# Gated linear attention with a channel mix on one Trainium2 core: five transfers of SyncE under way in place of eight, for the first 80

## The chip, the cores and the metric

One core of one Trainium2 chip runs the whole kernel. The metric is device time in microseconds (us) of one execution. TensorE is called PE here (PEld for its weight loads), VectorE DVE, ScalarE ACT, GpSimd POOL and SyncE SP. SP computes nothing: it begins DMA transfers, one after the other, in the order of its instructions.

## The reference, cut to what matters

```python
def _attn_ref(q, k, v, f_logit):                 # (4, 8, 768, 48) each
    f = 1.0 / (1.0 + np.exp(-f_logit))
    for t in range(S):
        state = f[:, :, t, :, None] * state + np.einsum('bhd,bhe->bhde', k[:, :, t], v[:, :, t])
        y[:, :, t] = np.einsum('bhd,bhde->bhe', q[:, :, t], state)
    return y

def _moe_ref(x, mu_k, mu_r, w_k, w_v, w_r):      # x: y as (4, 768, 384)
    xk = mu_k * x + (1.0 - mu_k) * x_prev        # x_prev: x one step earlier in time
    xr = mu_r * x + (1.0 - mu_r) * x_prev
    k = np.maximum(xk @ w_k, 0.0)                # 384 x 1024
    v = k * k @ w_v                              # 1024 x 384
    r = 1.0 / (1.0 + np.exp(-(xr @ w_r)))        # 384 x 384
    return r * v
```

The three weight matrices arrive as float64.

## The kernel before

The 4 x 768 time steps are cut into 24 chunks of 128 steps. A chunk is six jobs or more on each engine: its gates are turned into running sums of logarithms, its queries and keys are scaled by them, PE makes the scores and the products with the state, and ACT or DVE brings the result out of PSUM. Three chunks make a unit (eight units, u0 to u7), which then goes through the channel mix: the mix of neighbouring steps (`d`, `xm`), the products with w_k (`F0.0` to `F0.7` for unit 0), the squares, the products with w_r (`R`) and with w_v (`W`), the sigmoid, and the output. Every number that the channel mix multiplies is split into a high and a low part (`xh`, `xl`; `h`, `l`), so each product is three matmuls.

The float64 weights are loaded as pairs of 32-bit words, piece by piece (`wk0` to `wk7`, `wr0` to `wr3`, `wv0` to `wv5`). DVE turns a piece into float32 with three instructions (lines L678, L687 and L690), ACT rounds the high part (L693) and POOL subtracts for the low part (L697). Unit 0 can't start its products before the first pieces of w_k are there.

All of this is one list of tasks in a fixed order: the string `ORDER` names them one by one, `f0.0 sf0.0 cst zT0 ...`, and `emit` (L810) walks through it. Each task's instructions go to one engine, and `emit` ties each instruction to the one before it on its engine, so that no engine's order can change. Waits between engines follow from the tiles that the tasks write and read and are put in by the Tile framework. Transfers are tasks too: `f` (gates, L460), `qk` (a chunk's queries and keys, L234), `v` (values, L236), the weight pieces (L684), `mu` (L773), `sp` (SBUF to SBUF, `x<-stage`, L505), `out` (L652) and `c` (weight words read once more for a check, L745). All but the last output are begun by SP.

The first 30 transfers of SP, in order, are: f0.0, wr2, wk2, wr0, f0.1, f0.2, qk0, f1, wv1, v0, qk1, wk3, v2, wk0, wk4, mu, v1, qk2, wr3, wk6, qk3, wv2, v3, wk1, f2, qk4, wv0, wr1, v4, qk5. The text counts them so: the 8th transfer is f1, the 18th qk2. The 31st is the first `x<-stage`, for unit 0.

The framework gives the transfers of SP eight semaphores in turn, and a transfer that takes a semaphore waits until the one that had it before has landed. So the k-th transfer is begun no earlier than the landing of the (k-8)-th.

A second way of computing (`general`) is in the program for inputs with very strong gates. It doesn't run on these inputs, and its lists are emitted with `pinned=False`.

Of the kernel before, what the change touches and what calls it, by code (L numbers as in the profile page):

```python
# [45 lines left out]
WORDS = {"wk": (-0.282, 0.023), "wr": (-4.892, 0.005), "wv": (-0.241, 0.052)}  # L46
TIED = 6
QUARTER = 8
BUNDLE = True
AWAY = 1  # L50
HALVED = 1
# [145 lines left out]
class Rwkv:  # L197
# [22 lines left out]
    def add_attention(self, pl, i):  # L220
# [13 lines left out]
        pl.add(f"qk{i}", ga - 0.3, ("Q", 1.42, 1, lambda: nc.sync.dma_start(self.qk_t[i % NQ], self.qkt[i])),  # L234
               after=I("SP", i - NQ) + [f"{'QT' if i - NQ >= QUARTER else 'TR'}{i - NQ}"] * (i >= NQ) + I("YB", i - NQ) + late)
        pl.add(f"v{i}", at - 0.3, ("Q", 0.52, 1, lambda: nc.sync.dma_start(self.b("v", i), self.vt[i])),  # L236
# [116 lines left out]
        kq_in = lambda: self.py[:, :, 256:].rearrange("p r (a c) -> p a r c", a=NP)[:, :, :, :D]  # L353
        if i >= QUARTER:
            pl.add(f"QT{i}", at, ("P", 0.24, 0, quarters),
                   after=I("k") + [f"y{i - 3}"] + ([f"kt{i - 1}"] if i > QUARTER else []))
            pl.add(f"kt{i}", at, ("A", 0.5, 0, lambda: nc.scalar.copy(self.b("ktk", i), kq_in())),
# [54 lines left out]
        def y_state(p):  # L412
            for j in range(NP):
                for r in (0, 1):
                    s = r ^ p ^ j % 2
                    if cs > 0 or s == 1:
                        y_mm(j, r, r ^ p, self.z_t[i % 2][s][HALF[r], j], q()[HALF[r], j, HALF[s]], False)
# [8 lines left out]

        near = I("kt", i + 1) + I("q", i + 1) + I("m") + I("T") if BUNDLE and TIED <= i < N - 1 else []
        near = near + ([f"QT{i + 2}"] if QUARTER <= i + 2 < N else [])
        pl.add(f"YA{i}", at, ("P", 0.22, 0, lambda: y_state(1)), after=I("za") + I("zb") + I("q") + I("y", i - 1) + near)
# [379 lines left out]

    def emit(self, order, pinned=True):  # L810

        done, last = self.nc.cur_bb.bb.instructions, {}
        for _, way, self.slot in order:
            at = len(done)
            way[3]()
            for ins in done[at:] if pinned else ():
                if ins.engine in last:
                    self.tc.add_manual_dep(
                        ins, last[ins.engine],
                        mybir.DependencyInfo(mybir.DependencyClass.NoSync, mybir.DependencyReason.DATA),  # L820
                        reason="order on one engine",
                    )
                last[ins.engine] = ins.name
# [186 lines left out]
```

## Time and profile before

| | |
|---|---|
| median of 3 runs | 341.58 us (341.3 to 341.67) |
| the profiled execution | 341.73 us |
| its span, from the first to the last instruction | 339.9 us |
| granted clock of TensorE, mean | 0.999 |
| PE busy | 320.8 us (94% of the span) |
| DVE, ACT, POOL busy | 255.5, 205.2, 153.4 us |
| moved by DMA | 45.24 MB, mean 133 GB/s |

The span is what the rows below are measured in, from 0 at the first instruction. The execution's own time is 1.83 us more than its span.

### The profile page before, as it was taken

Reading aid. Unit: us, or ns where it says so; the run is one execution under the profiler, and the core shown is the slowest. Engines: PE = TensorE matmul, PEld = TensorE weight load, DVE = VectorE, ACT = ScalarE, POOL = GpSimd, SP = SyncE. Lnnn points to the kernel's source line nnn. Section 1 sums busy time; section 2 is a strip of 40 time slices with the busy share of each in tenths; the row PEclk is TensorE's granted clock in tenths of the full one; section 3 lists DMA queues with packets and bytes.
Section 4 is the critical chain, followed back from the end, with each engine's and each line's share of the span. In section 5 each row is a group of like instructions: output and inputs, shape, how many; then the busy total and the mean of one; then the engine's idle time right before and its main releaser. Section 6 shows DMA issues by size and latency. Waiting matters only on the chain. (4 is left out here: it accounts for less than half of the span.)

```text
span 339.9 us, 10992 instructions
## 1 busy us (share of the span) xinstructions
PE 320.8 (94%) x4574; PEld 304.5 (90%) x4574; DVE 255.5 (75%) x519; ACT 205.2 (60%) x432; POOL 153.4 (45%) x194
## 2 busy tenths in 40 slices
PE   4795889999999999999999999999999999999993
PEld 4675678899999999999999999999999999999993
DVE  5997999999988987686998886787475627837420
ACT  3888788784887736783658648591858236133420
POOL 2369589847762435313653356525612405214300
PEclk9999999999999999999999999999999999999999
DMA  7999667015465234470257122541520133040002
GB/s 230 398 385 360 185 193 273 14 29 158 175 198 152 75 97 153 102 267 25 87 125 269 62 46 85 170 143 60 187 91 5 32 117 92 35 141 23 0 4 79
DMA packets 20347, 45.24 MB, mean 133 GB/s; under 512 B 2752, under 2 KB 12736, under 8 KB 20288
## 3 DMA queue, kind: packets, MB, share of 16 engines
q1 hardware_dynamic: 20144, 44.25, 39.4%
q8 instruction: 38, 0.62, 0.8%
q10 hardware_dynamic: 144, 0.20, 0.2%
q14 instruction: 21, 0.17, 0.2%
HBM read 38.54 MB, written 4.72 MB: 127 GB/s over the span
## 5 line engine op out<-in xcount | busy, mean ns | idle before, releaser
L558 PE MATMUL pm<-xh,wk 128*128 128x384 f32 x384 | 103.5, 341 | 0.7 <-DVE words L690 0.5
L558 PE MATMUL pm<-wv,k2h 128*128 128x384 f32 x384 | 98.4, 338 | 0.0
L596 POOL TENSOR_TENSOR k2l<-kk,k2h 128x384 fp32r<-128x384 f32 x44 | 46.4, 1059 | 63.6 <-DVE kk L588 24.9
L558 PEld LDWEIGHTS pm<-xh,wk 128*128 128x128 f32 x384 | 69.8, 188 | 2.3 <-DVE words L690 0.6
L558 PEld LDWEIGHTS pm<-wv,k2h 128*128 128x128 f32 x384 | 69.0, 188 | 0.9 <-issue 0.5
L558 PE MATMUL pm<-wv,k2l 128*128 128x384 f32 x192 | 64.5, 336 | 0.4 <-issue 0.4
L558 PE MATMUL pm<-xl,wk 128*128 128x384 f32 x192 | 64.5, 336 | 0.0
L550 POOL TENSOR_TENSOR xl<-xm,xh 128x384 fp32r<-128x384 f32 x35 | 37.4, 1075 | 32.2 <-DVE xh L544 27.8
L289 POOL TENSOR_TENSOR qk<-qk,rb 128x256 f32<-128x256 f32 x23 | 17.1, 742 | 60.6 <-ACT rb L275 33.1
L586 ACT ACTIVATE k2h<-r 128x384 fp32r<-128x384 f32 x64 | 32.2, 519 | 12.8 <-DVE r L582 12.4
L558 PE MATMUL pm<-wr,xh 128*128 128x384 f32 x144 | 37.1, 339 | 0.3 <-DVE words L690 0.3
L558 PEld LDWEIGHTS pm<-wv,k2l 128*128 128x128 f32 x192 | 36.1, 188 | 0.0
L558 PEld LDWEIGHTS pm<-xl,wk 128*128 128x128 f32 x192 | 36.0, 188 | 0.0
L581 ACT ACTIVATE r<-pm 128x384 f32<-128x384 f32 x41 | 20.0, 488 | 24.5 <-PE pm L558 22.2
L558 PEld LDWEIGHTS pm<-wr,xh 128*128 128x128 f32 x144 | 25.8, 188 | 0.8 <-DVE words L690 0.6
L443 ACT ACTIVATE x<-py 64x128 f32<-64x128 f32 (+1 forms) x69 | 21.4, 310 | 8.1 <-PE py L410 4.9
L535 DVE SCALAR_TENSOR_TENSOR xm<-pm,mu_sb,x 128x384 f32<-128x384 f32 x42 | 24.9, 609 | 0.6
L270 DVE TENSOR_TENSOR_SCAN pm<-f,low 128x512 f32<-128x512 f32 x18 | 25.0, 1387 | 0.5 <-ACT f L624 0.3
L590 ACT ACTIVATE kk<-r 128x384 f32<-128x384 f32 x38 | 19.4, 519 | 9.6 <-DVE r L582 7.1
L558 PE MATMUL pm<-wr,xl 128*128 128x384 f32 x72 | 24.2, 336 | 0.0
L410 PE MATMUL py<-qk,z 64*64 64x64 f32 x704 | 21.6, 227 | 1.7 <-DVE z L330 0.9
L582 DVE TENSOR_SCALAR r<-pm 128x384 f32<-128x384 f32 x23 | 12.4, 549 | 12.8 <-PE pm L558 12.1
(129 smaller groups left out, 575.6 us busy)
## 6 DMA issues: line engine op xcount, KB each, us to landing
qk<-in_qkt SPq DMA_DIRECT2D x24, 512.0 KB, 5.6
words<-in_wv SPq DMA_DIRECT2D x12, 512.0 KB, 4.8
f<-in_zt SPq DMA_DIRECT2D x7, 768.0 KB, 6.7
v<-in_vt SPq DMA_DIRECT2D x24, 192.0 KB, 2.9
out<-o SPq DMA_DIRECT2D x23, 192.0 KB, 3.4
words<-in_wk SPq DMA_DIRECT2D x6, 512.0 KB, 5.0
words_k2l<-in_wk SPq DMA_DIRECT2D x4, 384.0 KB, 7.2
words_k2h<-in_wk SPq DMA_DIRECT2D x4, 384.0 KB, 7.6
```

Source lines behind the costliest of these rows:

```text
L270: pl.add(f"b{i}", ga, ("V", 1.25, 1, lambda: nc.vector.tensor_tensor_scan(b().rearrange(FL), f().rearrange(FL), self.low.rearrange(FL), 1. ...
L289: e.tensor_tensor(k()[:, ::2], k()[:, ::2], rb()[:, ::2], op=ALU.mult)
L410: first[c, h] = nc.tensor.matmul(to, lhs, rhs, start=(c, h) not in first, stop=stop, skip_group_check=True)
L443: e.activation(o, i_, AF.Copy, scale=sign)
L535: pl.add(f"xm{u}.{n}{j}", pr, ("V", 0.62, 0, lambda xm=xm, n=n, j=j: nc.vector.scalar_tensor_tensor(xm(), pm("d", u, j)[:, :UT], self.mu_s ...
L550: e.tensor_tensor(lo(), xm(), hi().bitcast(F32), op=ALU.subtract)
L558: nc.tensor.matmul(ps, lhs(a, j), rhs(bb, j), start=ends[0] and i == 0, stop=ends[1] and i == len(pr) - 1)
L581: pl.add(f"r{u}.{f}", kf, ("A", 0.5, 0, lambda r=r, ps=ps: nc.scalar.activation(r(), ps(), AF.Relu)), ("V", 0.56, 0, lambda r=r, ps=ps: nc ...
L582: ("V", 0.56, 0, lambda r=r, ps=ps: nc.vector.tensor_scalar(r(), ps(), 0.0, None, op0=ALU.max)),
L586: pl.add(f"h{u}.{f}", kf, ("A", 0.53, 0, lambda r=r, hi=hi: nc.scalar.activation(hi(), r(), AF.Square)), after=[f"r{u}.{f}"], **kw)
L590: ("A", 0.53, 0, lambda r=r, kk=kk: nc.scalar.activation(kk(), r(), AF.Square)),
L596: e.tensor_tensor(lo(), kk(), hi().bitcast(F32), op=ALU.subtract)
```

## The change

A counter `loads` is kept of the DMA instructions that SP issues. From the 6th to the 80th, each is given a dependency on the one five before it, of the class that makes the engine wait for its landing. Nothing else is changed: the order on every engine, the instructions and the tiles are the same.

```diff
+DEEP = 5
...
-        done, last = self.nc.cur_bb.bb.instructions, {}
+        done, last, loads = self.nc.cur_bb.bb.instructions, {}, []
         for _, way, self.slot in order:
             at = len(done)
             way[3]()
             for ins in done[at:] if pinned else ():
+                if "DMA" in type(ins).__name__ and ins.engine == self.nc.sync.engine:
+                    loads.append(ins.name)
+                    if DEEP < len(loads) <= 80:
+                        self.tc.add_manual_dep(
+                            ins, loads[-1 - DEEP],
+                            mybir.DependencyInfo(mybir.DependencyClass.Sync, mybir.DependencyReason.DATA),
+                            reason="transfers under way",
+                        )
                 if ins.engine in last:
```

## Rows read from the trace of the kernel before

**Rows 1.** The page: PE's busy tenths in 40 slices of 8.5 us.
```profile
PE   4795889999999999999999999999999999999993
```

**Rows 2.** Stretches: length, busy us and instructions of each engine, PE's clock, DMA share, GB/s.
```profile
7.00:34.91 27.91, 21.80 (x523) 18.02 (x521) 23.04 (x52) 22.57 (x51) 16.94 (x23) 1.00 0.98 370
34.91:47.16 12.25, 9.96 (x267) 7.89 (x266) 12.04 (x23) 9.17 (x21) 7.46 (x10) 1.00 0.68 219
47.16:340.00 292.84, 286.27 (x3778) 276.38 (x3778) 216.21 (x435) 170.62 (x358) 127.24 (x150) 1.00 0.33 105
```

**Rows 3.** SP in order of time: start, us, queue, line, transfer (8th, 12th, 30th, 31st).
```profile
4.53 0.46 SPq L460 DMA_DIRECT2D f<-in_zt  x1
...
8.07 0.57 SPq L684 DMA_DIRECT2D words_k2l<-in_wk  x1
...
26.11 0.33 SPq L234 DMA_DIRECT2D qk<-in_qkt  x1
32.23 2.52 SPq L505 DMA_DIRECT2D x<-stage  x4
```

**Rows 4.** Single transfers, KB and us from issue to landing: 1st, 4th, 8th, 15th, 16th, 17th, 25th.
```profile
f<-in_zt SPq DMA_DIRECT2D x1, 256.0 KB, 2.7
...
lg<-in_wr SPq DMA_DIRECT2D x1, 288.0 KB, 5.6
...
f<-in_zt SPq DMA_DIRECT2D x1, 768.0 KB, 8.0
...
words_k2h<-in_wk SPq DMA_DIRECT2D x1, 384.0 KB, 8.8
...
mu_sb<-in_mu SPq DMA_DIRECT2D x1, 3.0 KB, 7.1
...
v<-in_vt SPq DMA_DIRECT2D x1, 192.0 KB, 6.6
...
f<-in_zt SPq DMA_DIRECT2D x1, 768.0 KB, 8.9
```

**Rows 5.** DVE in order of time; in brackets the idle time before and what ended it.
```profile
6.61 0.56 DVE L678 TENSOR_SCALAR pm<-words_k2l 128x384 int32<-128x384 int32 x1 [0.87 <-DMA words_k2l<-in_wk]
8.15 0.46 DVE L678 TENSOR_SCALAR pm<-lg 128x288 int32<-128x288 int32 x1 [0.98 <-DMA lg<-in_wr]
...
12.52 1.02 DVE L463 TENSOR_SCALAR f<-f,sure 128x1536 f32<-128x1536 f32 x1 [0.56 <-DMA f<-in_zt]
...
28.08 0.36 DVE L330 TENSOR_TENSOR z<-pss,z 128x192 f32<-128x192 f32 x1 [0.79 <-PE pss L393]
...
34.50 0.36 DVE L330 TENSOR_TENSOR z<-pss,z 128x192 f32<-128x192 f32 x1 [1.98 <-POOL qk L290]
```

**Rows 6.** PE in order of time, up to the first product of the channel mix.
```profile
23.96 0.66 PE L344 MATMUL pm<-ident,qk 128*128 128x128 f32 x4
...
27.25 0.34 PE L373 MATMUL pss<-qk 64*64 64x64 f32 x8 [0.98 <-issue]
...
33.45 0.51 PE L373 MATMUL pss<-qk 64*64 64x64 f32 x19 [2.38 <-issue]
...
47.16 0.44 PE L558 MATMUL pm<-xh,wk 128*128 128x384 f32 x1 [0.48 <-DVE words L690]
```

**Rows 7.** A transfer of 192 KB into an empty queue: KB and us to landing.
```profile
out<-o SPq DMA_DIRECT2D x1, 192.0 KB, 1.9
```

**Rows 8.** POOL in order of time: the last wait for a chunk's queries and keys.
```profile
21.80 0.74 POOL L289 TENSOR_TENSOR qk<-qk,rb 128x256 f32<-128x256 f32 x1 [0.92 <-DMA qk<-in_qkt]
22.49 0.74 POOL L290 TENSOR_TENSOR qk<-qk,rb 128x256 f32<-128x256 f32 x1
```

**Rows 9.** The same stretch view: a slow stretch of the DMA and a full one.
```profile
3.75:7.00 3.25, 2.75 (x9) 2.24 (x10) 2.12 (x5) 1.57 (x3) 0.00 (x0) 1.00 0.93 262
8.00:11.50 3.50, 2.17 (x15) 1.58 (x15) 3.21 (x9) 2.10 (x4) 0.73 (x2) 1.00 1.02 407
```

**Rows 10.** DMA queues: kind, packets, MB, share of 16 engines.
```profile
q8 instruction: 38, 0.62, 0.8%
```

## The prediction

> **What bounds the kernel now.** I read the page first, then the stretches, then SP's order with the time of each transfer to its landing, and last the waits of DVE, PE and POOL in the start. On the page PE is full from the eighth slice on and has holes only in the first seven [rows 1]. The stretches say the same in numbers: from 47.16 to the end PE works 286.27 of 292.84 us, while in the 12.25 us before that it is DVE that is full, with 12.04 us [rows 2]. PE's first product of the channel mix, at 47.16, waits for DVE [rows 6]. So nothing that happens after 47 us is for a transfer queue to win or lose; the change counts by as much as it moves the 47.16.
>
> The start itself goes through the transfers and DVE. Up to 34.91 us the DMA is 98% busy at 370 GB/s [rows 2]. DVE waits for the landing of the 3rd, the 4th and the 8th transfer (0.87, 0.98 and 0.56 us), and after 12.52 it stands still for only 0.79 and 1.98 us in the list that I read, behind PE and POOL [rows 5]. Where PE stands still longest, at 27.25 and 33.45, its wait has no releaser ("issue"), and DVE's two late waits follow each of these by about a microsecond [rows 6, 5].
>
> That eight are under way today can be seen: the 12th transfer begins at 8.07 [rows 3]. The 4th, which is wr0, lands just then; DVE's first instruction on it starts at 8.15, straight out of its wait [rows 5].
>
> **The change, part by part.**
>
> *The waits themselves.* They are 75, on SP, and most find their transfer landed: after the 30th, SP's next issue is at 32.23 [rows 3], held by the unit's attention and not by the queue. A wait that is already satisfied costs nothing that I can see in SP's row of issues. I take 0; were each a tenth of the 0.33 us of an issue [rows 3], the six transfers of unit 0 would be 0.2 us later, which is the upper end.
>
> *The issues that move.* The 8th moves from 4.53 to the landing of the 3rd, 6.6 (DVE's wait for that ends at 6.61 [rows 5]), so by 2.1 us. The 12th moves from the landing of the 4th to that of the 7th. The largest move is the last: the 30th goes from 26.11 [rows 3] to the landing of the 25th. That one is f2; begun at 21.04 and 8.9 us on its way [rows 4], it lands at 29.9, so the 30th moves by 3.8 us. Behind it on SP stands the first `x<-stage`, which can't begin before 32.23 anyway [rows 3]: 2.3 us of cover. Of the later ones I find the 48th alone held, by about a microsecond; it is the queries and keys of chunk 8, and `ORDER` uses these only after F0.7, in the stretch where PE is full.
>
> *What a later issue costs at the landing.* A transfer that is begun into a queue with others in front waits in it: the 8th has 768 KB and takes 8.0 us, though at 370 GB/s its bytes are 2.1 us [rows 4, 2]. The later issue takes this time in the queue away, and the landing stays, as long as the four transfers in front last longer than the trip of a new one. The trip into an empty queue: 192 KB land 1.9 us after their issue [rows 7], of which the bytes at 407 GB/s [rows 9] are 0.5, so 1.4 us. The first transfer of all took 2.7 us for 256 KB [rows 4], by the same sum 2.0 us. The trip is thus 1.4 to 2.0. The thinnest cover is for the 17th and the 18th: in front of the 18th stand the 14th and 15th with 384 KB each (two pieces of w_k of one shape), the 16th with 3 and the 17th with 192 [rows 4], together 963 KB or 0.986 MB. At 407 GB/s [rows 9] this lasts 2.4 us, at 370 [rows 2] 2.7. It is 0.4 us more than the longer trip, so the queue doesn't run dry, and every other handover has at least that cover (the next thinnest are the 20th with 995 and the 19th with 1091 KB). Value taken: 0.
>
> The Trainium skill, in "DMA: Bandwidth & Descriptors" under "Anatomy of one DMA", gives about 2.0 us as the fixed part of a transfer, measured for transfers that GpSimd issues. By it the cover holds by the same 0.4 us; the rows of SP's own transfers, 1.4 and 2.0 us, agree.
>
> *What a shallower queue could give.* Two places. First, the stretch from 3.75 to 7.00 moves only 262 GB/s, against 407 a little later [rows 9]. Four issues (8th to 11th) fall in it today and would leave it. If it then ran at 407, its 0.85 MB would take 2.1 us, and the 4th and 8th would land up to 1.2 us earlier, and DVE with them. Against it: the stretch is slow from its beginning, before those four are issued, and from 8.00 to 11.50 the rate is 407 with eight under way and the 12th to 15th being issued. Taken: 0; upper end of the gain 1.2.
>
> Second, PE's instructions also come by DMA: 38 packets of 16 KB [rows 10]. PE's idle 0.98 and 2.38 us before 27.25 and 33.45 are ended by nothing in the program [rows 6], and I read them as waits for such a block. If a block has to pass what is queued, fewer transfers bring it sooner. At 27.25 the queue holds seven today and five after; at 33.45 it is down to five today as well (26th to 30th), so the second hole can't shrink by this. The gain is at most DVE's 0.79 at 28.08 [rows 5]. Taken: 0.
>
> The Trainium skill, in "Runtime: NRT & Kernel Launch" under "Instruction fetch mechanics", says that a sequencer refills its instructions in 16 KiB blocks by a DMA queue of its own and that this is mostly hidden. The size of the packets agrees with the trace; hidden it isn't here, if my reading of the two holes is right. In "DMA: Bandwidth & Descriptors" under "Queues, rings and completion order" it says that a DMA engine takes its queues in turn, packet by packet. By that rule a block waits for a packet and not for the whole queue, its wait is the same with five as with eight, and the gain of this place is 0.
>
> **The sum.** 0 for the waits, 0 for the landings, 0 for the two possible gains: the profiled execution's 339.9 us of span and 341.73 of time stay. Against the median of 341.58 the profiled one is 0.15 longer, so I forecast 341.5. About 0.2%, 0.7 us, is what a measurement of this kernel can tell from no change.
>
> **The rivals.**
>
> *Early transfers quicker.* As above, 1.2 us at most from the 262 GB/s stretch; half of that is inside what can't be told. For it: the slow stretch lies where SP issues without a pause. Against it: slow before, and full speed at 8.00. It would give 340.3 to 340.9. Chance 0.15.
>
> *Instruction blocks sooner.* 0.79 us from the first hole, 340.7; should the second hole shrink too, against my reading, DVE's 1.98 us are open as well, and 339.5 is possible. For it: these two are the only long waits of DVE after 12.52. Against it: five under way at the second hole before and after. Chance 0.17.
>
> *The queue runs dry (slower).* Place: the 17th to 20th transfers. It decides when a trip takes more than 2.4 us with the queue busy. The trace has one hint of longer trips: from the landing of the 3rd (6.6) to that of the 4th (8.07) it takes 1.5 us, and 288 KB at 407 GB/s are 0.7, so 0.8 us were lost in one transfer. With a trip of 2.0 + 0.8 = 2.8 us each of the four handovers loses up to 0.4 us, 1.6 in all at the 20th, and 0.8 at the 18th. POOL takes the 18th (qk2) as soon as it lands [rows 8], and PE turns POOL's result at 23.96 [rows 6], 0.7 us after POOL has ended (23.23). Of 0.8 us 0.1 would reach PE; with twice that loss 0.9, that is 342.4. Chance 0.13, about two thirds of it beyond 0.2%.
>
> *The change does nothing.* If the waits of the 6th to 80th are all met by the time SP gets there, issues stay where they are. The moves above exclude it for the 8th to 30th, but the time is the same as in the forecast.
>
> **How the numbers follow.** No change that can be told, by the forecast: 0.55. Early transfers 0.15, instruction blocks 0.17, dry queue 0.13. Of the two gains some 0.26 lie beyond 0.7 us, of the loss 0.09; from small shifts of any kind in a start where each engine's order is fixed I add 0.03 to either side. Faster 0.29, same 0.59, slower 0.12. The range takes in the likely part of both gains and the dry queue: 340.0 to 342.4. For no change alone it would be 341.2 to 341.9.
>
> **What the profile after would show.** SP's 8th issue at about 6.6, its 12th two to three microseconds after today's 8.07 and its 30th near 30; the same transfers landing within 0.3 us of today and their times to landing shorter by what the issue moved (the 8th about 6 in place of 8.0). 370 GB/s from 7 to 34.91 as now. DVE's waits of 0.87, 0.98 and 0.56 us as they are. PE's first product of the channel mix within 0.5 us of 47.16. I am wrong if that moves: earlier with DVE's early waits shrunk, it was the first gain; earlier with PE's two holes shrunk, the second; later, with DMA below full between 17 and 22 us, the queue ran dry.

## The result and the profile after

The changed kernel takes 343.02 us (median of 12 runs, 340.7 to 345.32), the kernel before 341.44 us beside it (12 runs, 340.27 to 342.76). The ratio is 1.0054, with a 95% interval of 1.0032 to 1.0076: slower, by 1.6 us between the two medians. The forecast was 341.5 us and no change, so it is wrong, and its range ends 0.6 us too low. The profiled execution has a span of 341.9 us, 2.0 more than before.

The page's slices of PE first; they hold the whole difference in the first seven.

```profile
PE   4687878999999999999999999999999999999993
```

Stretches of the changed kernel (columns as in [rows 2]):

```profile
3.75:7.00 3.25, 2.68 (x9) 2.17 (x10) 1.80 (x4) 1.53 (x3) 0.00 (x0) 1.00 0.85 233
8.00:11.50 3.50, 2.13 (x12) 1.44 (x12) 2.80 (x7) 1.70 (x4) 0.29 (x1) 1.00 0.94 348
7.00:34.91 27.91, 21.82 (x523) 18.16 (x522) 23.23 (x51) 21.62 (x51) 15.07 (x21) 1.00 0.96 345
47.10:66.00 18.90, 17.05 (x207) 15.39 (x208) 16.74 (x30) 14.43 (x36) 15.53 (x16) 1.00 0.55 193
...
20.00:24.00 4.00, 3.59 (x118) 3.08 (x117) 3.48 (x8) 3.91 (x11) 2.38 (x4) 1.00 0.84 299
```

The same stretch view of before, for the two stretches that were not shown:

```profile
20.00:24.00 4.00, 3.59 (x97) 3.19 (x97) 3.97 (x11) 3.45 (x9) 2.31 (x4) 1.00 1.05 403
...
47.10:64.10 17.00, 16.74 (x208) 15.47 (x209) 16.62 (x31) 14.50 (x36) 14.95 (x15) 1.00 0.49 164
```

With five under way the DMA moves 345 GB/s from 7 to 34.91 where it moved 370 [rows 2], and between 20 and 24 us, where it had been at 403, it moves 299 (share 0.84 against 1.05). From 7 to 34.91 the share falls only from 0.98 to 0.96, so little of that loss is idle time of the DMA engines. The stretches that begin at 47.10 say where the time goes: 207 matmuls behind the first product of the channel mix take 18.9 us, where 208 took 17.0.

SP in order of time (8th, 12th, 20th, 30th, 31st to 34th, 39th, 40th, 42nd transfer):

```profile
7.42 0.33 SPq L461 DMA_DIRECT2D f<-in_zt  x1
...
11.06 0.57 SPq L685 DMA_DIRECT2D words_k2l<-in_wk  x1
...
21.97 0.55 SPq L685 DMA_DIRECT2D words_k2l<-in_wk  x1
...
33.23 0.33 SPq L235 DMA_DIRECT2D qk<-in_qkt  x1
34.70 3.57 SPq L506 DMA_DIRECT2D x<-stage  x4
...
40.75 1.88 SPq L235 DMA_DIRECT2D qk<-in_qkt  x1
42.67 0.61 SPq L685 DMA_DIRECT2D words_k2h<-in_wk  x1
...
43.98 0.61 SPq L685 DMA_DIRECT2D words_k2l<-in_wk  x1
```

Before, the 30th began at 26.11 and the 31st at 32.23 [rows 3], the 39th, the 40th and the 42nd thus:

```profile
37.94 0.43 SPq L234 DMA_DIRECT2D qk<-in_qkt  x1
38.41 0.61 SPq L684 DMA_DIRECT2D words_k2h<-in_wk  x1
...
39.89 0.61 SPq L684 DMA_DIRECT2D words_k2l<-in_wk  x1
```

Single transfers of after, us from issue to landing (8th, 16th, 17th, 20th, 30th, 40th, 42nd):

```profile
f<-in_zt SPq DMA_DIRECT2D x1, 768.0 KB, 6.5
...
mu_sb<-in_mu SPq DMA_DIRECT2D x1, 3.0 KB, 5.2
...
v<-in_vt SPq DMA_DIRECT2D x1, 192.0 KB, 4.5
...
words_k2l<-in_wk SPq DMA_DIRECT2D x1, 384.0 KB, 4.5
...
qk<-in_qkt SPq DMA_DIRECT2D x1, 512.0 KB, 5.1
...
words_k2h<-in_wk SPq DMA_DIRECT2D x1, 384.0 KB, 5.3
...
words_k2l<-in_wk SPq DMA_DIRECT2D x1, 384.0 KB, 7.8
```

The times to landing of the first 30 are shorter, as foretold, but by less than the issues moved. Issue plus time to landing gives the landings: the 8th at 13.9 us (before 12.5), the 20th at 26.5 (before 16.64 + 6.8 = 23.5), the 30th at 38.3 (before 34.9, by the record of its semaphore).

DVE in order of time:

```profile
7.43 0.56 DVE L679 TENSOR_SCALAR pm<-words_k2l 128x384 int32<-128x384 int32 x1 [1.71 <-DMA words_k2l<-in_wk]
8.56 0.46 DVE L679 TENSOR_SCALAR pm<-lg 128x288 int32<-128x288 int32 x1 [0.57 <-DMA lg<-in_wr]
...
13.96 1.02 DVE L464 TENSOR_SCALAR f<-f,sure 128x1536 f32<-128x1536 f32 x1 [1.60 <-DMA f<-in_zt]
...
34.76 0.36 DVE L331 TENSOR_TENSOR z<-pss,z 128x192 f32<-128x192 f32 x1 [1.09 <-PE pss L394]
...
48.11 0.56 DVE L679 TENSOR_SCALAR pm<-words_k2h 128x384 int32<-128x384 int32 x1 [1.07 <-DMA words_k2h<-in_wk]
...
51.80 0.56 DVE L679 TENSOR_SCALAR pm<-words_k2l 128x384 int32<-128x384 int32 x1 [0.77 <-DMA words_k2l<-in_wk]
```

PE in order of time, those with a wait:

```profile
33.71 0.51 PE L374 MATMUL pss<-qk 64*64 64x64 f32 x19 [1.66 <-issue]
...
47.09 0.44 PE L559 MATMUL pm<-xh,wk 128*128 128x384 f32 x1 [0.61 <-DVE words L691]
...
49.77 0.44 PE L559 MATMUL pm<-xh,wk 128*128 128x384 f32 x1 [0.84 <-DVE xm L531]
59.03 0.41 PE L559 MATMUL pm<-xh,wk 128*128 128x384 f32 x1 [0.97 <-DVE bl L280]
```

Three things are to be seen here. The early waits grew (DVE's 0.56 for the 8th is 1.60 now [rows 5]). Yet PE's first product of the channel mix begins at 47.09, not later than the 47.16 before [rows 6]: the hole at 27.25 is gone, the one at 33 is 1.66 instead of 2.38 us, and DVE's waits of 0.79 and 1.98 at 28.08 and 34.50 became one of 1.09. A late start was swallowed where PE had stood still anyway. And behind 47 us stand two DVE waits that the kernel before doesn't have, for the 40th and the 42nd transfer (two pieces of w_k), and PE's waits of 0.84 and 0.97 follow them. The first product with w_r, `R0.0`, before:

```profile
63.40 0.45 PE L558 MATMUL pm<-wr,xh 128*128 128x384 f32 x1
```

and now:

```profile
65.39 0.44 PE L559 MATMUL pm<-wr,xh 128*128 128x384 f32 x1
```

So `F0.0` to `R0.0` takes 18.30 us instead of 16.24, and the rest of the span is 276.5 us in both. These 2.06 us, less 0.07 at `F0.0`, are the 2.0 of the span.

### The profile page after: what moved, and what is told of

Read it like the earlier page. It is cut to its first block, busy times and chain, and to the rows that moved or that the text cites. A ratio compares the mean times of both kernels' runs of the same rounds, so it can differ in the third digit from the quotient of the medians.

```text
span 341.9 us, 10991 instructions
## 1 busy us (share of the span) xinstructions
PE 321.2 (94%) x4574; PEld 304.5 (89%) x4574; DVE 254.8 (75%) x519; ACT 205.4 (60%) x432; POOL 153.0 (45%) x194
## 5 line engine op out<-in xcount | busy, mean ns | idle before, releaser
L411 PEld LDWEIGHTS py<-qk,z 64*64 64x64 f32 x704 | 15.7, 134 | 7.6 <-ACT stage L444 1.3
```

Of the source, the lines that this page charges most:

```text
L411: first[c, h] = nc.tensor.matmul(to, lhs, rhs, start=(c, h) not in first, stop=stop, skip_group_check=True)
```

## The experiments

Each is compared with runs of the kernel before on the same chip; "ratio" is that of the runs, with its 95% interval. A letter in an expectation names a theory. A: the thinned queue makes the transfers late, and this reaches PE through the 40th transfer. B: chance between executions. D: the loss arises where the fewest bytes are in front of a new transfer, at the 13th to 22nd. E: it takes both parts, the late transfers of the first 30 and the hold on the 31st to 38th. W: the short runs of w_k in memory are what the DMA engines are slow at.

**The change once more.** No edit.

> The changed kernel once more, for its spread. Theory A (each handover loses a little, so the queue delivers less from the 8th transfer on): the 30th transfer lands 2 to 4 us later than the 34.9 us of the kernel before, PE's first product of the channel mix is near 47 again, and the stretch up to unit 0's last rows is 1 to 2 us longer; 342.5 to 343.5 us. Rival B (the slow start of the profiled run, 3rd transfer at 7.4 and not 6.6 us, was chance and made the rest): with the 3rd landing at 6.6 the 30th lands near 35 and the time is near 341.6.

343.45 us, ratio 1.0071 [1.0042, 1.01]. `F0.0` at 46.44, `R0.0` at 64.66, the 30th landed at 37.6. DVE's wait:

```profile
48.09 0.56 DVE L679 TENSOR_SCALAR pm<-words_k2h 128x384 int32<-128x384 int32 x1 [1.70 <-DMA words_k2h<-in_wk]
```

The same wait at the same place, while `F0.0` is earlier still: B falls, although the 3rd landed at 7.0, between the two values that the expectation names.

**Only the first 30 held, and only those behind them.**

```diff
-                    if DEEP < len(loads) <= 80:
+                    if DEEP < len(loads) <= 30:     # one kernel
+                    if 30 < len(loads) <= 80:       # the other
```

> Only the 6th to 30th transfers are held to five under way; from the 31st on eight again. Theory A: the loads of the first 30 are late as with the whole change, so the w_k pieces behind them (40th and 42nd transfers) are late too: at least two thirds of the loss stays, ratio 1.003 to 1.006. Rival C (it is the hold on the 31st to 42nd, which keeps SP from beginning the transfers of unit 0 and the w_k pieces behind them): below 1.002.

> Only the 31st to 80th transfers are held to five under way; the first 30 as before. Theory A: the 30th lands at 34.9 us as before, nothing behind it is held long, ratio 0.999 to 1.001. Rival C: the loss of the whole change, 1.003 to 1.006.

341.08 us, ratio 0.9986 [0.9964, 1.0008], and 340.85 us, ratio 0.9998 [0.9976, 1.002]. By the runs neither part costs anything by itself. A alone doesn't foresee the first of these: late transfers of the first 30 were to be enough. (The profiled execution of the first, at 343.07, is among the longest of its runs, 339.8 to 343.23. Its 30th is issued at 34.67 and lands 4.8 us late, `F0.0` is at 49.34, and it has the slower clock told of in the last section. A very late 30th can thus cost without the second hold, by another way.)

**Four and six under way.**

```diff
-DEEP = 5
+DEEP = 4     # one kernel
+DEEP = 6     # the other
```

> Four under way in place of five, 6th to 80th as in the change. Theory A: each handover has one transfer less of cover, the rate from 7 us on falls from 345 to about 300 GB/s, the 30th lands 3 to 6 us later than with five, and the time is 345 to 348 us. Rival D (the loss sits only where the 3 KB and 192 KB transfers stand in the queue, 17th to 20th, and the rest has cover to spare): 343.5 to 344.5 us, with the rate between 8 and 15 us as with five.

> Six under way in place of five, 6th to 80th transfer otherwise as in the change. Five cost about 2 us and four 7. Theory A (the rate grows with what is under way until the engines are full): rate from 7 to 34.91 us between 355 and 365 GB/s, 30th landing about 36, DVE's waits for the w_k pieces (40th, 42nd) gone or under 0.3 us, 341.3 to 342.0 us. Rival (the loss comes from holding x<-stage behind loads at all, whatever the depth): 342.3 us or more.

With four 348.57 us, ratio 1.0199 [1.0169, 1.0229]; with six 341.72, ratio 1.0002 [0.9976, 1.0027]. The rate with four:

```profile
7.00:34.91 27.91, 21.55 (x468) 18.02 (x467) 21.37 (x48) 19.21 (x45) 12.43 (x16) 0.94 0.88 291
```

With six it is 374. So four, five, six and eight under way give 291, 345, 374 and 370 GB/s: down to six the rate stays, and below that each one less costs more. With four `F0.0` itself is late (54.17), the time is 0.6 us above what A allowed, and from 8.00 to 11.50, too, the rate is 291 (348 with five), so the loss isn't bound to the thinnest place.

**The hold taken from the 31st to 38th alone.**

```diff
-                    if DEEP < len(loads) <= 80:
+                    if DEEP < len(loads) <= 30 or 38 < len(loads) <= 80:
```

> Held are the 6th to 30th and the 39th to 80th transfers; the 31st to 38th (unit 0's x<-stage, v5 and wv3) are begun as in the kernel before. Theory E (the loss needs both: loads that land late, and the 31st to 38th begun one by one at their landings, so that the 40th and 42nd are begun late): most of the loss goes, ratio under 1.003. Rival F (it is the hold on the 39th to 42nd themselves): the loss stays, 1.005 to 1.007.

341.45 us, ratio 0.9991 [0.9965, 1.0018]. The first `x<-stage` and the 40th on SP:

```profile
32.32 2.51 SPq L506 DMA_DIRECT2D x<-stage  x4
...
38.85 0.61 SPq L685 DMA_DIRECT2D words_k2h<-in_wk  x1
```

From the 31st to the 40th this takes 6.5 us; in the changed kernel, where each `x<-stage` waits for one more landing of the first 30, 34.70 to 42.67 is 8.0, and before it was 32.23 to 38.41, 6.2. The 40th lands at 38.85 + 5.3 = 44.2, DVE doesn't wait for it, and the loss is gone: E holds. In this execution the first 30 were also less late than in the change (348 GB/s from 20 to 24 us, the 30th 1.9 us late and not 3.4); that E holds rests on the ratios of these three kernels and the change.

**Held from the 17th on.**

```diff
-                    if DEEP < len(loads) <= 80:
+                    if 16 < len(loads) <= 80:
```

> Held are the 17th to 80th; the first 16 are begun as in the kernel before. The profile of the change shows the rate low from 8 us on. Theory A (every handover loses): the 16th lands at 19.6 and not 22 us, the 30th about 1.5 us late and not 3.4, a third to two thirds of the loss stays: 1.002 to 1.0045. Rival D (the thin cover at the 17th to 20th makes it): the 30th is late by 3 us or more and the whole loss stays, 1.006 to 1.007.

343.0 us, ratio 1.0031 [1.0005, 1.0057]. The 30th lands 2.7 us late (37.6), the rate from 20 to 24 us is 256, and DVE waits 1.69 us at 47.41 for the 40th. The early moves (8th to 16th) are not needed for a loss. The ratio is in A's range and not in D's, and the lateness lies between the two, so this run doesn't decide.

**The hold taken from the 13th to 22nd alone, and its counterpart.**

```diff
-                    if DEEP < len(loads) <= 80:
+                    if DEEP < len(loads) <= 80 and not 12 < len(loads) < 23:    # one kernel
+                    if 12 < len(loads) < 23 or 30 < len(loads) <= 80:           # the other
```

> The change with the 13th to 22nd transfers begun as in the kernel before (eight under way); the 6th to 12th and the 23rd to 80th held to five. In every profile with five held over them the 15th and the 20th land 0.4 to 2.4 us later than their bytes explain, and the rate from 20 to 24 us is 234 to 299 GB/s. Theory D (the four transfers in front, with 3 KB and 192 KB among them, are too thin a cover there, since a trip is 3 to 5 us and not 2.4): rate from 20 to 24 us above 360, 30th landing within 1.2 us of 34.9, ratio 0.998 to 1.002. Rival A (any held stretch loses its share): 30th late by 1.5 us or more, ratio above 1.003.

> The reverse: only the 13th to 22nd and the 31st to 80th transfers are held to five. Theory D: rate from 20 to 24 us 240 to 300 GB/s, 30th landing 2 to 3 us late, DVE's wait for the 40th is there, ratio 1.003 to 1.007. Rival A: 30th late by 1 us or less, ratio under 1.002.

Without it 340.67 us, ratio 0.9992 [0.9972, 1.0012]; with it and the hold behind the 30th alone 342.28, ratio 1.003 [1.0011, 1.0049]. The stretch from 20 to 24 us of the one:

```profile
20.00:24.00 4.00, 3.85 (x124) 3.44 (x118) 3.93 (x11) 3.91 (x11) 2.81 (x4) 1.00 1.05 395
```

and of the other:

```profile
20.00:24.00 4.00, 2.98 (x80) 2.54 (x78) 3.93 (x11) 3.23 (x9) 2.01 (x3) 1.00 0.85 250
```

The slow stretch and the loss come and go together with these ten holds, as long as the hold behind the 30th stands: D holds for the place, though both lateness forecasts missed (the 30th 1.4 us late without these holds, 4.1 with them and the hold behind), and not every profile with five under way had the low rate that the expectation names (348 GB/s in the kernel with the 31st to 38th free). In the profile of the second the time is lost before `F0.0` (49.55; `F0.0` to `R0.0` is 16.05), so it doesn't show the way by the 40th. Part of its 4.1 us isn't the hold's either: SP's issue of the 23rd took 2.51 us there and ended 0.34 us behind a 16 KB packet of the instruction queue (last section).

**The short runs of w_k.** Its pieces lie in memory in short runs; here w_k is laid out so that each piece is one run of 3 KB for each partition, with the change and without it.

```diff
-                    return self.words[tag][:, :, h * P : (h + 1) * P]
+                    return self.words[tag][:, h]
...
-                piece("wk", 2 * i + h, home, view, lambda c=c: self.wk[:, :, c], [KJ, P],
+                piece("wk", 2 * i + h, home, view, lambda p=2 * i + h: self.wk[:, KJ * p : KJ * p + KJ], [KJ, P],
...
-        tag: k.turns.tile([P, KJ, 2 * P, 2], I32, name=f"words_{tag}", tag=tag) for tag in BUFS if tag.startswith("k2")
+        tag: k.turns.tile([P, 2, KJ, P, 2], I32, name=f"words_{tag}", tag=tag) for tag in BUFS if tag.startswith("k2")
...
-    wk = _words(inputs["moe_w_k"])[pt]
+    wk = _words(inputs["moe_w_k"])[pt].reshape(P, KJ, DFF // P, P).transpose(0, 2, 1, 3).reshape(P, -1, P)
```

> The change, with w_k laid out so that each of its eight pieces is one run of 3 KB per partition in HBM and in SBUF, and not three of 1 KB. Theory W (a w_k piece takes some 3.5 to 4 us from issue to landing even where nothing is in front of it, because it is 384 short runs, and the cover of four transfers is too thin for that): the 3rd transfer lands near 5.4 us in place of 6.6 to 7.4, the rate from 8 to 24 us is back above 380 GB/s, the 30th lands by 35.5, and the ratio is 0.994 to 1.001. Rival A (each handover loses whatever the runs are): rate still 345 to 355, ratio above 1.004.

> The kernel before with the same layout of w_k. Theory W: the 3rd transfer lands about 1.2 us earlier, DVE's waits of 0.87 and 0.98 us shrink, the later transfers were full already; 0 to 1.2 us faster, ratio 0.9965 to 1.000. Rival (the slow stretch from 3.75 to 7 us has nothing to do with the short runs): 3rd landing at 6.6 as before, ratio 0.999 to 1.001.

With the change 342.85 us, ratio 1.0024 [1.0008, 1.0041], and 273 GB/s from 20 to 24 us; without it 341.24, ratio 0.9983 [0.9961, 1.0005]. The 3rd landed at 7.6 us in both, not earlier. Long runs don't fill the gap: W falls. A had asked for more than 1.004 with the change, which the median misses.

**Five single holds taken away**, those of w_k's pieces, and five of others beside them.

```diff
-                    if DEEP < len(loads) <= 80:
+                    if DEEP < len(loads) <= 80 and len(loads) not in (12, 14, 15, 20, 24):    # one kernel
+                    if DEEP < len(loads) <= 80 and len(loads) not in (11, 13, 16, 19, 23):    # the other
```

> The change, but the five w_k pieces among the held loads (12th, 14th, 15th, 20th, 24th) are begun without the wait for the fifth before. Theory W: these are what the queue runs out on, the 30th lands within 1 us of 34.9 and the ratio is 0.999 to 1.002. Rival A: five of 25 waits less give back about a fifth, 1.004 to 1.006.

> The control for the run with the w_k pieces free: five other transfers (11th, 13th, 16th, 19th, 23rd; qk1, v2, mu, wr3, v3) are begun without the wait, the w_k pieces keep it. Theory W: little is given back, 1.004 to 1.007. Rival (any five waits less do the same): the same ratio as with the w_k pieces free.

342.41 us, ratio 1.0024 [0.9999, 1.0048], and 341.78, ratio 1.0018 [0.9994, 1.0043]: not told apart from each other, nor for certain from no change. The first lies between W's range and A's, the second below W's; in their profiles the 30th lands 2.8 and 5.5 us late. In the first the 20th lands at 23.6, as early as before, but the gap then stands in front of the 21st (28.0), and DVE waits 2.61 us for the 40th. That the gap moves to the next held transfer speaks for the queue and against w_k.

**The two pieces of w_k begun ahead of the queries**, with the change and without it.

```diff
-... sp0.1 d0.02 wv3 qk6 wk5 qk7 wk7 d0.00 ...
+... sp0.1 d0.02 wv3 wk5 wk7 qk6 qk7 d0.00 ...
```

> The whole change, and in the order of SP's transfers the two w_k pieces wk5 and wk7 go ahead of the queries and keys qk6 and qk7 (39th and 40th in place of 40th and 42nd). Theory G (the loss reaches PE only through DVE's waits of 1 to 1.7 and 0.8 us for these two pieces): they land 1.3 and 2.5 us earlier, both waits go, and the ratio falls to 0.998 to 1.002. Rival H (the start as a whole is late, the two waits are only where it shows): the time stays within 0.5 us of the change's, 1.005 or more.

> The kernel before with wk5 and wk7 ahead of qk6 and qk7, the control for the run of the change with that order. The kernel before has no wait of DVE for these two pieces, so by theory G nothing is to be had: 0.998 to 1.002. If the order by itself were worth something, the ratio would be under 0.998.

With the change 342.76 us, ratio 1.0015 [0.9983, 1.0048]: too wide to tell. Without it 342.0, ratio 1.0024 [1.0, 1.0048]: the order by itself brings no gain. The profile of the first is plainer: with these two pieces ahead DVE has no wait for either, and `F0.0` to `R0.0` is 47.73 to 63.74, 16.0 us as before the change. So in this execution the 2 us behind `F0.0` go with these two landings; its `F0.0` is 0.6 us later than in the change, at the lower clock (0.79 from 34 to 42 us).

None of these versions is shown to be faster than the kernel before.

## Why the prediction was wrong

**The step that failed** is the trip of a new transfer, in "What a later issue costs at the landing". The prediction took 1.4 to 2.0 us, from transfers into an empty queue, and set them against a cover of 2.4 us or more. The cover was right where it can be read: in front of the 20th it had reckoned 995 KB, 2.5 us, and the 20th was issued at 21.97, 2.5 us ahead of the landing of the 19th (19.97 + 4.5). But the 20th landed at 26.5, 2.0 us behind the 19th, where its own bytes take 1.0 at 407 GB/s. Its trip, bytes left out, was thus 21.97 to 25.5, 3.6 us. The same sum (landing, less the bytes, less the issue, where the landing comes later than the bytes after the one in front) gives 3.8 us at the 14th, 5.2 at the 15th and 4.6 at the 8th, which is no piece of w_k; in the change once more 5.2 at the 15th and 4.1 at the 20th. So a transfer begun while the DMA engines are busy needed some 4 us, about twice the time into an empty queue, and the four in front didn't always last that long.

The trace's records of single packets say where these microseconds are (only pieces of w_k have packets of 1024 bytes). The first packet of the 20th starts 1.3 us after its issue, and it lands 0.4 us after its last one starts: together 1.7 us, inside the prediction's 1.4 to 2.0. But from its first packet to its last it takes 2.8 us, for bytes worth 1.0. In the kernel before the 20th takes 2.6 us from first to last as well, behind a deeper queue, where nothing is lost by it. The prediction reckoned as if a transfer's packets ran one behind the other at the full rate.

The packets also get slower. From 7 to 34.91 us 12 packets of the loads took over 0.3 us before (4.5 us in sum), 67 in the changed kernel (35.1 us in sum, over 16 engines), 26 with six under way and 111 with four. They lie where the hold is: from 15 to 26 us there is 1 before, 1 where the 13th to 22nd are free, 19 in the changed kernel, and 42 where of the first 30 only the 13th to 22nd are held. So over the start as a whole the DMA engines worked more slowly rather than stood idle; why a packet takes longer with fewer behind it, no run shows.

The profile of before had a row for this: the 3rd transfer, begun at 1.73 with two in front, needed 4.9 us, and 3.9 without its bytes (first packet after 2.0 us, last after 4.5). In the list of single transfers of before (columns as in [rows 4]):

```profile
words_k2l<-in_wk SPq DMA_DIRECT2D x1, 384.0 KB, 4.9
```

The prediction used from the same region only the 0.8 us that the 4th lost, as a surcharge on the trip of the rival. It had the row nearest to the disputed case, a transfer begun while others run, and took the one from the empty queue.

The Trainium skill, in "DMA: Bandwidth & Descriptors" under "Latency and other measured facts", says that the latency of the memory is 0.2 us on average and 2 us at high load and makes up most of a transfer's fixed part. The 1.7 us that the 20th takes outside its packets stay within that figure; the 2.8 us between its first packet and its last are not covered by it.

**The rival that came nearest** was the dry queue, given a chance of 0.13. Its sign for it was right (DMA below full between 17 and 22 us: 264 to 379 GB/s there by the microsecond, and the least, 186, from 23 to 24), its place nearly so (17th to 20th; losses stand at the 8th, 14th, 15th, 20th and 21st). Its price (0.9 us) and its way to the end were wrong. It sent the loss through qk2, POOL and PE at 23.96. The lateness adds up so: 1.4 us at the 8th (13.9 against 12.5), 3.0 at the 20th, 3.4 at the 30th. What reached `F0.0` of it was swallowed by PE's holes.

**The cover of 2.3 us at the 31st** was put at the right place and then counted as whole, since the landings were to stay. With landings 3.4 us late, the 31st was held until 34.70, 2.5 us later, and the chain from the 31st to the 40th took 1.8 us more. Up to the 36th, where most wait for one more landing, it lost 1.1 us. The other 0.7 are no wait of the change: SP's issue of the 39th lasts 1.88 us, where before it was 0.43, while the 36th lasted 1.23; both end 0.4 us behind a 16 KB packet of the instruction queue (last section). How much of DVE's wait would be left without these 0.7 us was not tested. The 40th began 4.3 us later and landed 2.8 us later (48.0 against 38.41 + 6.8 = 45.2). DVE came to it at 47.03 before, so 1.8 us were covered, and the 1.07 us left are the wait in the row above. DVE before, at the two pieces:

```profile
47.03 0.55 DVE L678 TENSOR_SCALAR pm<-words_k2h 128x384 int32<-128x384 int32 x1
...
49.86 0.55 DVE L678 TENSOR_SCALAR pm<-words_k2l 128x384 int32<-128x384 int32 x1
```

The profiled executions with five under way and holds in both parts line up with such a cover (the kernel with the other order left out). Where the 30th lands 1.4 us late the execution takes 341.8 us, as before the change; 2.7 to 2.8 late (four executions) 342.6 to 343.1; 3.4 (the change) 343.7; 4.1 343.8; 5.5 344.6. The ratios of the runs don't line up with the lateness in the one profile: 2.7 us go with 1.0031 in one kernel and with 1.0071 in the change once more, 5.5 with 1.0018. The lateness differs between executions of one kernel (3.4 and 2.7 us in the two of the change), so it is to be compared with the time of its own execution.

**Two sentences were wrong outright.** "So nothing that happens after 47 us is for a transfer queue to win or lose": the stretch row said 286.27 us of work in 292.84, but DVE's order from 47.03 on had pieces of w_k that had landed only 1.8 and 2.4 us ahead of their use. And "Of the later ones I find the 48th alone held": the holds on the 31st to 38th are what carries the loss over. A smaller reading was wrong too: at 33.45 the queue of the kernel before is not "down to five (26th to 30th)"; the 26th to 28th have landed by 33.20. That was so at 31.07, where the hole begins.

**What was right.** The waits themselves cost nothing that shows (with six under way, 74 of them, the ratio is 1.0002). The early stretch didn't become quicker, it went from 262 [rows 9] to 233 GB/s. The 8th began at 7.42 (6.6 was forecast) with 6.5 us to landing (about 6). PE's first product stayed within 0.5 us of 47.16, but as a sum of two changes that the prediction hadn't foreseen: a later 8th, and smaller holes of PE. Its reading of these holes as waits for instructions fits the packets. The 16 KB packet of the instruction queue that goes with the second hole ends at 32.08 before and at 32.41 now, and PE goes on 1.37 and 1.30 us behind it. So the rival of instruction blocks sooner didn't happen: the block came 0.3 us later, and the hole shrank because PE reached it later, at 32.05 and not 31.07.

**What stays open.** Why packets spread and slow down with fewer transfers under way, and whether the time goes to one of the 16 DMA engines or to all, can't be read from these views. Apart from the kernel with four under way, in four profiled executions (the first 30 held; the 13th to 22nd held; five others free; w_k in long runs) `F0.0` itself is late, at 48.9 to 49.6 us, and the stretch behind it is as before or, with five others free, 1.2 us longer. All four have the lower clock in 34 to 42 us (0.59 to 0.79). But the kernel before with the two pieces ahead has `F0.0` at 48.41 with no hold at all, also at 0.79, so a late `F0.0` isn't by itself a sign of late transfers. How often the loss takes this way was not measured.

## What to carry to other kernels

To judge a limit on transfers under way, compare what is in front of a new transfer with its time to landing under load; take that time from a transfer that was begun while others ran, not from one into an idle queue. Then don't stop at the engine that is full: list, for the first stretch behind the start, how long ahead of its use each weight landed, since these few microseconds of cover are what a late queue eats. And two edits that each cost nothing alone can cost together, when the one uses up the cover of the other. Last, one profiled execution is one draw: set its lateness beside its own time and not beside the median of the runs.

## What was not expected of the hardware

Down to six transfers of some 0.4 MB under way the rate doesn't fall (374 GB/s, 370 with eight); below that it does: 345 with five (321 to 363 over five profiles that hold the first 30 so), 291 with four.

PE's long waits without a releaser go with its instructions. In the 17 profiles there are 33 such holes of over 0.6 us between 15 and 52 us, and each ends 1.26 to 1.64 us behind the end of a 16 KB packet of the instruction queue. SP has the same: issues that last 1.1 us and more, where others take 0.3 to 0.6, mostly end 0.34 to 0.39 us behind such a packet (the 39th of the changed kernel at 42.63, the packet at 42.25). I read both as waits for code; the packets don't say which engine they are for. So a long row of SP need not be a wait for the queue.

TensorE's granted clock falls to its lower level (1.2 GHz) behind PE's long hole in some executions and not in others. In the kernel that holds the 13th to 22nd, whose PE stood still for 2.94 us until 34.10:

```profile
32.00:34.00 2.00, 0.00 (x0) 0.00 (x0) 0.77 (x2) 1.97 (x5) 2.00 (x4) 0.85 0.98 376
34.00:36.00 2.00, 1.90 (x54) 1.81 (x55) 0.23 (x1) 1.99 (x2) 1.17 (x3) 0.50 0.95 369
36.00:38.00 2.00, 2.00 (x20) 1.14 (x20) 1.97 (x6) 1.72 (x3) 2.00 (x3) 0.50 0.37 129
38.00:40.00 2.00, 2.00 (x8) 1.62 (x7) 1.97 (x5) 0.55 (x1) 1.44 (x4) 0.50 0.09 24
40.00:42.00 2.00, 2.00 (x14) 1.51 (x12) 1.93 (x5) 1.10 (x3) 1.50 (x2) 0.95 0.47 131
```

The third column from the end is the clock: 0.50 for six microseconds (34 to 40), then nearly full again. The two profiles of before and after have 1.00 there, with holes of 2.38 and 1.66 us; with six under way a hole of 2.38 did lower it (0.79 on average from 34 to 42 us). This isn't the cause of the loss: where the change was run once more, the mean clock over the runs was 0.992 for it and 0.992 for the kernel before beside it.
